# Fourier mixing, a dense layer and routed experts on one core: the experts as one list of token groups, routing in finer steps

## The chip, the cores and the metric

The kernel runs on one core of a Trainium2 chip. Its engines take their own queues of instructions: TensorE (PE in the profile) makes matrix products into PSUM banks, VectorE (DVE), ScalarE (ACT) and GpSimd (POOL) work element by element, SyncE (SP) issues most loads. ACT and POOL issue DMAs too. The metric is the device time of one execution in microseconds (us); the number compared is the median of several runs.

## What is computed

```python
def reference(x, w_r, w_i, b_r, b_i, moe_w_in, moe_w_out, w_gate, w1, w2, capacity):
    X = np.fft.rfft(x, axis=1)                                # x: 8 x 3072 x 256
    Yr = X.real @ w_r - X.imag @ w_i + b_r
    Yi = X.real @ w_i + X.imag @ w_r + b_i
    Y = shrink(Yr, 0.01) + 1j * shrink(Yi, 0.01)              # soft threshold
    y = np.fft.irfft(Y, n=3072, axis=1).reshape(-1, 256)
    h = y @ moe_w_in                                          # 256 -> 2048
    t = np.where(h > 0, h, np.exp(np.minimum(h, 0)) - 1) @ moe_w_out
    logits = t @ w_gate                                       # 8 experts
    e = logits.argmax(1); gate = softmax(logits)[e]
    # in token order an expert takes its first `capacity` = 768 tokens, the rest give 0
    out[i] = gate[i] * (np.maximum(t[i] @ w1[e], 0) @ w2[e])  # 256 -> 1024 -> 256
```

Products are made in split form: each operand is a sum of two narrower numbers, and three products stand for one.

## The kernel before

Three stages follow each other and overlap at their seams. The **Fourier stage** (to about 250 us) transforms and mixes three batches; its last inverse products (`fi`, line 268, taken out of PSUM by ACT as `yt`, line 269) run on beside the dense stage. With this data 55 tiles of 128 tokens fill all experts, so that only these are worked on (a tail for other data follows behind a branch that is not taken here).

The **dense stage** (class `Moe`) takes the 55 tiles as 14 chunks, 13 of four tiles and a last one of three, and 16 steps a chunk: 224 dense steps, counted by `g` in the main loop. A step is `up` (six products `pa`, line 453, of 512 columns, 384 in the last chunk) for step `g` and `down` (twelve products `pm`, line 476, nine in the last chunk) for step `g - 3`. Between them ACT makes two activations `e` (457, 458), DVE the third `e` (459), ACT the first half `g` (460) and DVE, or POOL in some steps, the second half (461). The PSUM banks of `pa` are three, and the DVE `e` frees one. At a chunk's end ACT copies `pm` to `row` (484).

**Routing** of a chunk is the generator `finish(c)`: each `next` on it puts down one portion. It makes 32 `lw` on DVE (504: one logit of 128 tokens each), then small DVE operations `mx`, `eq`, `sb`, `qi` and `oh` (515 to 522, the choice of the expert), `bf` and `al` on POOL (528: sums over the tiles), then three small products `pk` on PE (538, 539: places of the tokens), which take a bank of the three called `pd`, shared with `pm` of odd chunks, `fi` and the turns of the experts. From `pk` DVE makes `pg`, `cnt` (the running counts) and at last `sl`, by which POOL scatters the rows of each tile to the table `tab` in DRAM (helper line 395). For the last chunk the third tile is computed aside: POOL makes two `pr` (498) and ACT eight `la` from them (501), since the PE no longer needs ACT as much there.

The **expert stage** (class `Experts`) has eight experts of 768 rows, two groups of three tiles each. `load_x` loads an expert's rows `er` from `tab` through SP; `turn` transposes a tile on PE (`eturn`, 626) and splits it into two `ex` (ACT 628, DVE 629); `up` makes eight `eup` per group (646, six products each), from which ACT and DVE make `eh` (647, 648); `down` makes three `edown` (659, 24 products each), from which ACT makes `eo` (662), scattered by POOL to `out`. `split_w` splits the loaded weights `ewraw` into `ew` (606, 607) and issues a later load. `pieces` lists all of an expert's `up` of both groups, then its six `down`, with the splits and turns of the next expert between them.

The order on each engine is set by a scheduler that goes over the pieces as the loop emits them and moves instructions within reach of it; each engine then runs its list in that order. So the place of `next(steps)` or of a piece in the loop decides, but not alone.

Of the kernel before, what the change touches and what calls it, by code (L numbers as in the profile page):

```python
# [10 lines left out]
F32 = mybir.dt.float32  # L11
F32R = mybir.dt.float32r
BF16 = mybir.dt.bfloat16
I32 = mybir.dt.int32
# [24 lines left out]

W_AT, ROW_AT, TURN_AT = 7, 10, 4  # L40
LAG = 3
RW = 258
# [371 lines left out]
class Moe:  # L414
# [70 lines left out]

    def finish(self, c):

# [6 lines left out]
        for t in range(2, nt) if aside else ():  # L494

            for q in (0, 4):
# [59 lines left out]
class Experts:  # L556
# [53 lines left out]

    def load_x(self, e):
        t = self.tile("row", [128, self.st, RW], F32, "er")
        rows = self.tab[bass.ds((self.at + e) * self.slots, self.slots), :]
        load(self.tc, t, rows.rearrange("(t p) w -> p t w", p=128))
        self.row[e] = t

    def turn(self, e, g, t):

        nc = self.nc
        a, n = self.groups[g]  # L620
        if t == 0:
            pool = next(self.pools["x"])
            self.xt[e, g] = [pool.tile([128, 2, n * 128], F32R, name=f"ex{r}") for r in (1, 2)]
        ps = self.bank("turn", [128, 2, 128])
        for dh in range(2):
            nc.tensor.transpose(ps[:, dh, :], self.row[e][:, a + t, dh * 128:dh * 128 + 128], self.id)  # L626
# [23 lines left out]
    def down(self, e, g, t):  # L650
        nc = self.nc
        a = self.groups[g][0] + t
# [7 lines left out]
        row = self.row[e]  # L660
        o = self.tile("o", [128, D], F32, "eo")
        nc.scalar.activation(o, ps, AF.Copy, scale=row[:, a, D:D + 1])  # L662
        scatter(self.tc, "out", self.out, row[:, a, D + 1:D + 2].bitcast(I32), o, NT, self.free)

    def pieces(self, experts):

        out, ng, last = [], len(self.groups), experts[-1]
        turns = lambda e: [lambda g=g, t=t: self.turn(e, g, t) for g in range(ng) for t in range(self.groups[g][1])]
        for e in experts:
            todo = []  # L670
            if e < last:
                todo += [lambda e=e, i=i: self.split_w(e + 1, i) for i in range(4)]
                todo.insert(0 if e == experts[0] else len(todo), lambda e=e: self.load_x(e + 1))
                todo += turns(e + 1)
            first = e == experts[0]
            if first:
                out += turns(e)
                self.hold = todo[0] if todo else None
            n = 0
            for g in range(ng):  # L680
                for f in range(NFE):
                    out.append(lambda e=e, g=g, f=f: self.up(e, g, f))
                    n += 1
                    if first and todo and n == W_AT:
                        out.append(lambda: [self.load_w(q) for q in range(4, 7)])
                    if todo and (n > ROW_AT and len(todo) > len(turns(e)) if first else f % 2):
                        out.append(todo.pop(0))
            for g in range(ng):
                for t in range(self.groups[g][1]):
                    for _ in range(1 if not first else 0 if g * self.groups[0][1] + t < TURN_AT else 2):  # L690
                        if todo:
                            out.append(todo.pop(0))
                    out.append(lambda e=e, g=g, t=t: self.down(e, g, t))
            out += todo
        return out


@with_exitstack
def kernel(ctx, tc, x, w_r, w_i, b_r, b_i, moe_w_in, moe_w_out, w_gate, w1, w2, cst, out, cap):
# [154 lines left out]
    n = n_static * NF  # L854
    z0 = n // 3

    ex = Experts(tc, w1, w2, tab, out, slots, rt["id"])
# [4 lines left out]
    for g in range(n + 16):  # L862
# [14 lines left out]
        if not todo and left is not None:  # L877
            left.close()
            left = None
            pools = {m: [mk(fast, "e0_" + m, b)] * b for m, b in dict(raw=3, w=1, row=1, x=1, h=1).items()}  # L880
            tags = dict(turn=["pd"], up=["pa"], down=["pb", "pc"])
# [17 lines left out]
        if sp0 and g % 4 == 3:  # L899
            sp0.pop(0)()  # L900
        if g == n:

            snap = rtp.tile([1, 1], I32, name="snap")
            nc.vector.tensor_scalar(snap, rt["cnt"][0:1, 0:1], float(cap), None, op0=ALU.is_lt)
            ex.load_x(0)
            spx = ex.pieces(range(E))
        if g == n + LAG:
            mst.close()
            right.close()
            for m, b in dict(w=1, row=1, x=2, h=1, o=4).items():  # L910
                pools[m] = [mk(fast, "e1_" + m, b, side="right")] * b + pools.get(m, [])
            ex.phase(ps, tags, **pools)
            mp["pr"] = mk(fast, "e1_pr", 2, side="right")
        c -= 1
        if c >= 0 and f >= LAG:
            if f == LAG:
                steps = moe.finish(c)
            next(steps, None)
            if c == n_static - 2 and f == 5 or c == n_static - 1 and f > 5:
                next(steps, None)  # L920
        for _ in range(2):
            if g >= n + LAG and (spx[0] is not ex.hold or f > 10):
                spx.pop(0)()
    for _ in steps:
        pass
# [4 lines left out]
    nc.vector.tensor_tensor(more, more, snap, op=ALU.max)  # L930
    for piece in spx:
        piece()
    fast.close()
    with tc.If(nc.values_load(more[0:1, 0:1], min_val=0, max_val=1) > 0):
        tail(tc, mk, rt, (x, w_r, w_i, b_r, b_i, cst), (zs[0], vs[0], ys[0]), (moe_w_in, moe_w_out), tab, cap, slots)
        with tc.For_i(0, E, 1) as e, ExitStack() as again:
            pools = {m: [mk(again, "r_" + m, b)] * b for m, b in dict(raw=3, w=1, row=1, x=2, h=2, o=2).items()}
# [5 lines left out]
            ex.load_x(0)  # L943
            for i in range(4):
                ex.split_w(0, i)
            for piece in ex.pieces([0]):
                piece()
# [96 lines left out]
```

## Time and profile before

| | us |
|---|---|
| median of three runs (1234.79 to 1238.55) | 1236.99 |
| the profiled execution, its own time | 1233.33 |
| its span, first to last instruction | 1231.4 |
| PE busy | 1167.1 |
| DVE busy | 835.3 |
| ACT busy | 717.7 |
| POOL busy | 294.3 |
| mean granted clock of PE | 0.981 |

Busy time of an engine is the sum of its instructions. PE is close to the span, so one reads where it was idle and who ended that idle time (its releaser). A second thing to read is the granted clock of a stretch: 1.00 is 2.4 GHz, 0.50 is 1.2 GHz, and a stretch with a value between spent a part of its time at the lower level.

### The profile page before, as it was taken

The numbers are of one execution on the slowest core, as the hardware profiler recorded it, in microseconds if no ns is written. First come the engines' busy times: TensorE is split into PE (matmuls) and PEld (weight loads), VectorE is DVE, ScalarE is ACT, GpSimd is POOL, SyncE is SP. The second block draws the span as 40 slices with busy tenths as digits, with TensorE's granted clock in tenths as the row PEclk, the third lists the DMA queues.
The fourth block names the chain that finished last, engine by engine and source line by source line (L and its number), as shares of the span: only waits on it lengthen the run. The fifth ranks groups of instructions, "written<-read, shape, count | busy, mean of one in ns | idle before, by whom it ended". The sixth has DMA issues, their size and how long they took to land.

```text
span 1231.4 us, 20925 instructions
## 1 busy us (share of the span) xinstructions
PE 1167.1 (95%) x7656; PEld 1061.6 (86%) x7656; DVE 835.3 (68%) x2140; ACT 717.7 (58%) x1397; POOL 294.3 (24%) x335
## 2 busy tenths in 40 slices
PE   7888898999999999999999999999997999999994
PEld 2676798889999989999998899999987999999994
DVE  1699889873868768668588787788787544355430
ACT  4565676666666666666667566666655544355430
POOL 1234334311131231321212312312222111111111
PEclk9999998999999999999999999999998999999998
DMA  8965887555120211333424223212103522332100
GB/s 267 315 221 173 241 256 219 173 162 170 48 67 27 74 50 40 121 108 97 137 84 145 72 69 121 95 56 83 62 8 97 198 101 92 105 112 99 45 26 29
DMA packets 122784, 143.65 MB, mean 117 GB/s; under 512 B 8962, under 2 KB 106099, under 8 KB 122544
## 3 DMA queue, kind: packets, MB, share of 16 engines
q1 hardware_dynamic: 72688, 77.62, 20.8%
q10 hardware_dynamic: 45040, 51.96, 12.5%
q0 software_dynamic: 4944, 12.64, 2.9%
q8 instruction: 62, 1.02, 0.3%
q14 instruction: 50, 0.41, 0.1%
HBM read 71.96 MB, written 71.15 MB: 116 GB/s over the span
## 4 chain that ended last, share of the span: by engine, by line
PE 65%; DVE 8%; issue 4%; ACT 2%; DMA 2%; POOL 1%; POOLq 0%; SPq 0%; ACTq 0%; DVEq 0%
PE pm L476 22%; PE pa L453 22%; PE eup L646 9%; PE edown L659 8%; DVE lw L504 3%; PE fi L268 2%; DVE e L459 1%; DVE tc L237 1%; PE eturn L626 1%; POOL out L395 1%; DMA ewraw<-in_moe_w 1%; DVE g L461 1%; PE fmix L226 0%; ACT e L458 0%; PE fi L245 0%
## 5 line engine op out<-in xcount | busy, mean ns | idle before, releaser
L476 PEld LDWEIGHTS pm<-wout,g 128*128 128x128 f32 x2640 | 347.4, 192 | 18.3 <-ACT e L457 0.7
L476 PE MATMUL pm<-wout,g 128*128 128x256 f32 x2640 | 353.9, 283 | 0.5 <-DVE g L461 0.5
L453 PE MATMUL pa<-x,win 128*128 128x512 f32 (+1 forms) x1344 | 347.8, 394 | 1.0 <-DVE e L459 0.6
L453 PEld LDWEIGHTS pa<-x,win 128*128 128x128 f32 x1344 | 238.5, 190 | 38.9 <-DVE e L459 1.0
L460 ACT CAST g<-e 128x512 fp32r<-128x512 f32 (+1 forms) x224 | 136.7, 612 | 148.8 <-DVE e L459 147.9
L504 DVE SCALAR_TENSOR_TENSOR lw<-row,wg 128x256 bf16<-128x256 f32 x432 | 210.0, 486 | 12.1 <-ACT row L484 4.4
L459 DVE SCALAR_TENSOR_TENSOR e<-pa,e 128x512 f32<-128x512 f32 (+1 forms) x224 | 151.0, 677 | 86.4 <-ACT e L458 85.8
L461 DVE TENSOR_TENSOR g<-e,g 128x512 fp32r<-128x512 f32 (+1 forms) x182 | 139.3, 768 | 55.6 <-ACT g L460 53.6
L457 ACT ACTIVATE e<-pa 128x512 f32<-128x512 f32 (+1 forms) x224 | 132.4, 591 | 55.0 <-PE pa L453 54.1
L458 ACT ACTIVATE e<-e 128x512 f32<-128x512 f32 (+1 forms) x224 | 139.3, 625 | 4.9
L646 PE MATMUL eup<-ex,ew 128*128 128x384 f32 x768 | 141.3, 341 | 0.1
L659 PE MATMUL edown<-ew,eh 128*128 128x256 f32 x1152 | 139.8, 280 | 0.8 <-ACT eo L662 0.8
L659 PEld LDWEIGHTS edown<-ew,eh 128*128 128x128 f32 x1152 | 136.2, 188 | 1.0 <-ACT eo L662 1.0
L461 POOL TENSOR_TENSOR g<-e,g 128x512 fp32r<-128x512 f32 (+1 forms) x42 | 53.7, 1280 | 341.5 <-ACT g L460 302.4
L646 PEld LDWEIGHTS eup<-ex,ew 128*128 128x128 f32 x768 | 133.4, 189 | 1.6 <-DVE eh L648 0.6
L648 DVE SCALAR_TENSOR_TENSOR eh<-eup,eh 128x384 fp32r<-128x384 f32 x128 | 70.5, 555 | 54.0 <-ACT eh L647 53.9
L395 POOL DMA_INDIRECT out<-eo,er x48 | 46.6, 971 | 220.7 <-ACT ex L628 136.7
L647 ACT ACTIVATE eh<-eup 128x384 fp32r<-128x384 f32 x128 | 63.2, 494 | 57.6 <-PE eup L646 56.2
L237 DVE SCALAR_TENSOR_TENSOR tc<-tt,kb 64x256 f32<-64x256 f32 x144 | 81.6, 567 | 14.8 <-ACT kb L232 12.5
L607 DVE TENSOR_TENSOR ew<-ewraw,ew 128x512 fp32r<-128x512 f32 x64 | 42.1, 686 | 61.4 <-ACT ew L606 49.7
L662 ACT ACTIVATE eo<-edown,er 128x256 f32<-128x256 f32 x48 | 22.8, 475 | 94.3 <-PE edown L659 62.9
L395 POOL DMA_INDIRECT tab<-row,sl x55 | 57.7, 1050 | 51.7 <-DVE sl L551 39.2
(124 smaller groups left out, 1237.3 us busy)
## 6 DMA issues: line engine op xcount, KB each, us to landing
out<-row ACTq DMA_DIRECT2D x48, 512.0 KB, 3.4
ewraw<-in_moe_w SPq DMA_DIRECT2D x29, 512.0 KB, 4.5
xp<-in_x SPq DMA_DIRECT2D x24, 384.0 KB, 5.0
zs<-zo ACTq DMA_DIRECT2D x24, 384.0 KB, 4.0
zi<-zs SPq DMA_DIRECT2D x36, 256.0 KB, 5.1
vs<-vo ACTq DMA_DIRECT2D x36, 256.0 KB, 3.7
vi<-vs SPq DMA_DIRECT2D x48, 192.0 KB, 3.7
y<-ys SPq DMA_DIRECT2D x26, 256.0 KB, 3.4
```

Of the source, the lines that this page charges most:

```text
L237: nc.vector.scalar_tensor_tensor(c[b, j, :], t[a, r, :], 0.0, kb[a, r, :], op0=ALU.max, op1=ALU.subtract)
L395: i = tc.nc.gpsimd.indirect_dma_start(dst, bass.IndirectOffsetOnAxis(idx, 0), src, None, bounds_check=rows - 1, oob_is_err=False)
L453: nc.tensor.matmul(ps, l, r, start=n == 0, stop=n == len(ops) - 1)
L457: nc.scalar.activation(e, ps, AF.Exp)
L458: nc.scalar.activation(e, e, AF.Relu, bias=1.0, scale=-1.0)
L459: nc.vector.scalar_tensor_tensor(e, ps, 0.0, e, op0=ALU.max, op1=ALU.subtract)
L460: nc.scalar.copy(g1, e)
L461: (nc.gpsimd if f % 4 == 3 and f < NF - 1 else nc.vector).tensor_tensor(g2, e, f32(g1), op=ALU.subtract)
L476: nc.tensor.matmul(self.pm[c][h][:, o, :], l[:, ts], r[f // 2][:, f % 2, :], start=f == 0 and o == 0 and n == 0, stop=f == NF - 1 and (o = ...
L504: v.scalar_tensor_tensor(T("lw", [128, D], BF16), row[:, t, 0:D], 1.0, rt["wg"][:, e, :], op0=ALU.mult, op1=ALU.mult, accum_out=pl[:, t, e ...
L646: nc.tensor.matmul(ps, l, r, start=i == 0, stop=i == len(ops) - 1)
L659: nc.tensor.matmul(ps, l[:, f, ts], r[:, f, :], start=f == 0 and i == 0, stop=f == NFE - 1 and i == 2)
```

## The change

Three things, all in the order and the size of the pieces.

- `finish(c, per)` yields after every three `lw` (four in the last three chunks) in place of eight, so that a chunk's routing lasts longer and reaches into the next chunk's; a list `live` holds the routings under way and each is stepped once per dense step.
- The experts' work is one list over 16 groups. `load_x` loads the rows of one group (387 KB in place of 774 KB, two buffers). The three `down` of a group stand among the eight `up` of the next one, with the turns of the group after that and two splits; each piece has a cost (`up` 1, `down` 3, others 0) and the loop emits 2 per step.
- The handover: twelve steps before the dense stage ends the rows of expert 0 are loaded, and the three turns of its first group stand at the steps `n - 8`, `n - 5`, `n - 2`. The rows of group (1,1), the second of expert 1, are the first that must wait for every chunk's routing (`hold`). Two counters are kept at the early load, so that data for which the early load would be too early goes to the tail.

```diff
-    def finish(self, c):
+    def finish(self, c, per=E):
...
-        for t in range(nt):
-            for e in range(E) if t < 2 or not aside else ():
-                v.scalar_tensor_tensor(T("lw", [128, D], BF16), row[:, t, 0:D], 1.0, rt["wg"][:, e, :],
-                                       op0=ALU.mult, op1=ALU.mult, accum_out=pl[:, t, e:e + 1])
-            yield
+        last = (2 if aside else nt) * E - 1
+        for n in range(last + 1):
+            t, e = divmod(n, E)
+            v.scalar_tensor_tensor(T("lw", [128, D], BF16), row[:, t, 0:D], 1.0, rt["wg"][:, e, :],
+                                   op0=ALU.mult, op1=ALU.mult, accum_out=pl[:, t, e:e + 1])
+            if n % per == per - 1 or n == last:
+                yield
...
-    def load_x(self, e):
-        t = self.tile("row", [128, self.st, RW], F32, "er")
-        rows = self.tab[bass.ds((self.at + e) * self.slots, self.slots), :]
+    def load_x(self, e, g):
+        a, n = self.groups[g]
+        t = self.tile("row", [128, self.groups[0][1], RW], F32, "er")[:, 0:n, :]
+        rows = self.tab[bass.ds((self.at + e) * self.slots + a * 128, n * 128), :]
...
     def pieces(self, experts):
...
+        todo = [(e, g) for e in experts for g in range(len(self.groups))]
+        size = lambda k: self.groups[todo[k][1]][1]
...
+        out, self.hold = turns(0), None
+        for k, (e, g) in enumerate(todo):
+            side = {f: [] for f in range(NFE)}
+            if k + 1 < len(todo):
+                rows = (0, lambda k=k: self.load_x(*todo[k + 1]))
+                late = k == 2
+                if late:
+                    self.hold = rows
+                if k:
+                    side[ROW_AT if late else 0].append(rows)
+                for t, f in enumerate(turns(k + 1)):
+                    side[NFE - 1 if late else NFE - 1 - size(k + 1) + t].append(f)
+                split = []
+                if g == len(self.groups) - 1:
+                    split = [(e + 1, 0), (e + 1, 1)]
+                elif g == 0 and k:
+                    split = [(e, 2), (e, 3)]
+                for n, q in enumerate(split):
+                    side[2 * n + 1].append((0, lambda q=q: self.split_w(*q)))
+            for f in range(NFE):
+                out.append((1, lambda e=e, g=g, f=f: self.up(e, g, f)))
+                out += side[f]
+                if k and f % 3 == 1:
+                    t = f // 3
+                    if t < size(k - 1):
+                        out.append((3, lambda k=k, t=t: self.down(*todo[k - 1], t)))
...
+    TURN_AT = [n - 8, n - 5, n - 2]
+    live = []
...
-        if g == n:
-            snap = rtp.tile([1, 1], I32, name="snap")
-            nc.vector.tensor_scalar(snap, rt["cnt"][0:1, 0:1], float(cap), None, op0=ALU.is_lt)
-            ex.load_x(0)
+        if g == n - NF + LAG + 1:
+            while len(live) > 1:
+                step(0)
+            snap = rtp.tile([1, 2], I32, name="snap")
...
+            for q in range(len(ex.groups)):
+                ex.load_x(0, q)
             spx = ex.pieces(range(E))
...
-        if c >= 0 and f >= LAG:
-            if f == LAG:
-                steps = moe.finish(c)
-            next(steps, None)
-            if c == n_static - 2 and f == 5 or c == n_static - 1 and f > 5:
-                next(steps, None)
-        for _ in range(2):
-            if g >= n + LAG and (spx[0] is not ex.hold or f > 10):
-                spx.pop(0)()
+        for q in range(len(live)):
+            step(0)
+        if c >= 0 and f == LAG:
+            live.append(moe.finish(c, 3 if c < n_static - 3 else 4))
+            step(-1)
+        if c == n_static - 1 and f > 5:
+            step(-1)
+        if g == n - 8:
+            for q in range(4, 7):
+                ex.load_w(q)
+        room = 2 if g >= n else g in TURN_AT
+        while room > 0 and spx and (spx[0] is not ex.hold or not live):
+            cost, piece = spx.pop(0)
+            piece()
+            room -= cost if g >= n else 1
```

Three places show what the scheduler makes of it. Line numbers of after run two or three higher. PE, the `pk` of chunk 12 (the last chunk but one): before, inside the `up` of the last chunk's fourteenth step, with six `down` still to come.

```order
L453 MATMUL pa<-x,win_79 128x384 x2
L538 LDWEIGHTS u
L538 MATMUL pk<-oh,u 128x32
L453 MATMUL pa<-x,win_80 128x384
L538 LDWEIGHTS one
L538 MATMUL pk<-bf,one 128x32
L476 MATMUL pm<-wout_1795,g_10928 128x256
```

And after, behind the `down` of the last dense step but one:

```order
L476 MATMUL pm<-wout_1799,g_11047 128x256
L540 LDWEIGHTS u
L540 MATMUL pk<-oh,u 128x32
L540 LDWEIGHTS one
L540 MATMUL pk<-bf,one 128x32
L541 LDWEIGHTS one
L541 MATMUL pk<-al,one 128x8
L649 MATMUL eup<-ex_10868,ew_7677 128x384
```

It moved from the fourteenth `up` of the last chunk to the end of its `down`, among the first `eup`.

DVE, the last `lw` of chunk 12, which lie beside the dense steps of the last chunk (`e` frees a bank of `pa`, `g` is its second half). Before:

```order
L459 SCALAR_TENSOR_TENSOR e<-pa,e 128x384
L504 SCALAR_TENSOR_TENSOR lw,pl<-row,wg 128x256 x2
L461 TENSOR_TENSOR g_10929<-e,g_10928 128x384
L504 SCALAR_TENSOR_TENSOR lw,pl<-row,wg 128x256
L459 SCALAR_TENSOR_TENSOR e<-pa,e 128x384
L504 SCALAR_TENSOR_TENSOR lw,pl<-row,wg 128x256 x2
L515 TENSOR_REDUCE mx<-pl 128x4
```

After:

```order
L505 SCALAR_TENSOR_TENSOR lw,pl<-row,wg 128x256 x4
L459 SCALAR_TENSOR_TENSOR e<-pa,e 128x384
L505 SCALAR_TENSOR_TENSOR lw,pl<-row,wg 128x256
L632 TENSOR_TENSOR ex_10869<-eturn,ex_10868 128x2x128
L461 TENSOR_TENSOR g_10839<-e,g_10838 128x384
L505 SCALAR_TENSOR_TENSOR lw,pl<-row,wg 128x256 x10
L517 TENSOR_REDUCE mx<-pl 128x4
L518 TENSOR_TENSOR eq<-pl,mx 128x32
L519 TENSOR_TENSOR sb<-pl,mx 128x32
L522 TENSOR_TENSOR eq<-eq,e_2362 128x32
L523 TENSOR_REDUCE qi<-eq 128x4
L524 TENSOR_TENSOR oh<-qi,e_2362 128x32
```

One or two `lw` stood between two operations of the dense step; now ten stand together, and the next `e` behind `oh`.

ACT in the handover, where `row` of the last chunk, the `la` of its third tile, `ex` of the turns and `eh` of the first `eup` meet. Before:

```order
L484 COPY row<-pm 128x256
L501 ACTIVATE la,pl<-pr 128x256 x2
L628 CAST ex_11187<-eturn 128x2x128
L501 ACTIVATE la,pl<-pr 128x256
L628 CAST ex_11187<-eturn 128x2x128
L501 ACTIVATE la,pl<-pr 128x256
```

After (here `ex` is that of the second group of expert 0; `pr` stands on POOL right behind the four scatters of chunk 12 in both):

```order
L650 ACTIVATE eh_11103<-eup 128x384 x2
L501 ACTIVATE la,pl<-pr 128x256
L650 ACTIVATE eh_11103<-eup 128x384
L501 ACTIVATE la,pl<-pr 128x256 x2
L631 CAST ex_11183<-eturn 128x2x128
L501 ACTIVATE la,pl<-pr 128x256
L631 CAST ex_11183<-eturn 128x2x128
L501 ACTIVATE la,pl<-pr 128x256
L631 CAST ex_11183<-eturn 128x2x128
```

`la` stood among the `ex` of the first group and now stands among those of the second, with `eh` of the first between them.

## Rows read from the trace of the kernel before

**Rows 1.** Windows of 25 us: busy us per engine (instructions), clock, DMA share, GB/s.
```profile
675.00:700.00 25.00, 21.73 (x126) 18.98 (x125) 21.02 (x69) 14.38 (x26) 7.26 (x10) 0.93 0.18 62
...
900.00:925.00 25.00, 22.18 (x149) 21.46 (x147) 18.30 (x69) 13.46 (x29) 7.19 (x11) 0.93 0.06 14
925.00:950.00 25.00, 18.16 (x105) 16.89 (x106) 20.97 (x71) 12.45 (x38) 8.59 (x8) 0.86 0.27 96
```

**Rows 2.** PE waits, 250 to 1231 us: line, releaser, total, times, longest.
```profile
PE eturn L626 <- DVE ex L629: 3.9, 1, 3.9
PE pk L538 <- DVE oh L522: 3.8, 2, 2.2
PE eturn L626 <- DMA er<-tab: 2.8, 1, 2.8
PE pk L538 <- ACT yt L269: 2.3, 1, 2.3
PE pk L538 <- POOL bf L528: 1.9, 3, 1.1
...
PE edown L659 <- ACT eo L662: 0.8, 1, 0.8
```

**Rows 3.** Timeline of PE, 885 to 892 us: start us, us, what, shapes, count.
```profile
886.58 1.21 PE L453 MATMUL pa<-x,win 128*128 128x384 f32 x6
887.62 1.59 PE L476 MATMUL pm<-wout,g 128*128 128x256 f32 x12
889.05 1.21 PE L453 MATMUL pa<-x,win 128*128 128x384 f32 x6
```

**Rows 4.** Chain of waits behind three holes: start us, us, what.
```profile
693.40 2.37 PE pa L453 x6
...
914.94 1.28 PE pm L476 x8
916.22 1.92 PE pa L453 x6
...
935.27 3.06 PE eup L646 x15
...
938.56 4.26 PE eup L646 x24
```

**Rows 5.** Chain of waits on DVE, 909 to 914 us.
```profile
909.34 0.47 DVE g L461
...
911.00 0.44 DVE lw L504 x2
...
913.25 0.11 DVE oh L522
```

**Rows 6.** Chain of waits, 943 to 975 us.
```profile
948.81 2.32 DMA tab<-row,sl
...
951.73 5.59 DMA ewraw<-in_moe_w
...
965.65 2.83 PE edown L659 x24
```

**Rows 7.** Timeline of POOL, 911 to 934 us; idle time ahead in brackets.
```profile
917.00 1.06 POOL L395 DMA_INDIRECT tab<-row,sl  x1 [2.09 <-DVE sl L551]
...
920.92 1.01 POOL L395 DMA_INDIRECT tab<-row,sl  x1 [0.30 <-issue]
925.62 4.82 POOL L498 TENSOR_TENSOR pr<-wg,row 128x1024 f32<-128x1024 f32 x2 [3.69 <-ACT row L484]
```

**Rows 8.** Costliest groups of the page: busy us, mean ns, idle ahead.
```profile
L648 DVE SCALAR_TENSOR_TENSOR eh<-eup,eh 128x384 fp32r<-128x384 f32 x128 | 70.5, 555 | 54.0 <-ACT eh L647 53.9
...
L607 DVE TENSOR_TENSOR ew<-ewraw,ew 128x512 fp32r<-128x512 f32 x64 | 42.1, 686 | 61.4 <-ACT ew L606 49.7
```

**Rows 9.** Timeline of ACT, its first `la`.
```profile
927.99 0.42 ACT L501 ACTIVATE la<-pr 128x256 bf16<-128x256 f32 x1 [2.45 <-POOL pr L498]
```

**Rows 10.** Timeline of DVE beside the first `pr`.
```profile
925.77 2.47 DVE L504 SCALAR_TENSOR_TENSOR lw<-row,wg 128x256 bf16<-128x256 f32 x1
```

More of the change, by code (lines that the diff above doesn't have):

```diff
@@ L659, in down @@
                 nc.tensor.matmul(ps, l[:, f, ts], r[:, f, :], start=f == 0 and i == 0, stop=f == NFE - 1 and i == 2)
-        row = self.row[e]
+        row = self.row[e, g]
         o = self.tile("o", [128, D], F32, "eo")
-        nc.scalar.activation(o, ps, AF.Copy, scale=row[:, a, D:D + 1])
-        scatter(self.tc, "out", self.out, row[:, a, D + 1:D + 2].bitcast(I32), o, NT, self.free)
+        nc.scalar.activation(o, ps, AF.Copy, scale=row[:, t, D:D + 1])
+        scatter(self.tc, "out", self.out, row[:, t, D + 1:D + 2].bitcast(I32), o, NT, self.free)
@@ L665, in pieces @@
     def pieces(self, experts):
[L667 to L694, printed above, removed]
@@ L695, in pieces, with turns @@
-        return out
+        todo = [(e, g) for e in experts for g in range(len(self.groups))]
+        size = lambda k: self.groups[todo[k][1]][1]
+        def turns(k):
+            return [(0, lambda t=t: self.turn(*todo[k], t)) for t in range(size(k))]
+        out, self.hold = turns(0), None
[24 more added lines that the diff above has]
+                        out.append((3, lambda k=k, t=t: self.down(*todo[k - 1], t)))
+            if k:
+                out += [(3, lambda k=k, t=t: self.down(*todo[k - 1], t)) for t in range(3, size(k - 1))]
@@ L698 @@
+        k = len(todo) - 1
+        return out + [(3, lambda t=t: self.down(*todo[k], t)) for t in range(size(k))]
 @with_exitstack
@@ L855, with step @@
     z0 = n // 3
+    TURN_AT = [n - 8, n - 5, n - 2]
+    live = []
+    def step(i):
+        if live:
+            s = live.pop(i)
+            if next(s, live) is not live:
+                live.append(s)
     ex = Experts(tc, w1, w2, tab, out, slots, rt["id"])
@@ L879 @@
             left = None
-            pools = {m: [mk(fast, "e0_" + m, b)] * b for m, b in dict(raw=3, w=1, row=1, x=1, h=1).items()}
+            pools = {m: [mk(fast, "e0_" + m, b)] * b for m, b in dict(raw=3, w=1, row=2, x=1, h=1).items()}
             tags = dict(turn=["pd"], up=["pa"], down=["pb", "pc"])
@@ L909 @@
             right.close()
-            for m, b in dict(w=1, row=1, x=2, h=1, o=4).items():
+            for m, b in dict(w=1, row=2, x=2, h=1, o=4).items():
                 pools[m] = [mk(fast, "e1_" + m, b, side="right")] * b + pools.get(m, [])
@@ L914 @@
         c -= 1
-        if c >= 0 and f >= LAG:
-            if f == LAG:
-                steps = moe.finish(c)
-            next(steps, None)
-            if c == n_static - 2 and f == 5 or c == n_static - 1 and f > 5:
-                next(steps, None)
-        for _ in range(2):
-            if g >= n + LAG and (spx[0] is not ex.hold or f > 10):
-                spx.pop(0)()
-    for _ in steps:
-        pass
+        for q in range(len(live)):
[13 more added lines that the diff above has]
+            room -= cost if g >= n else 1
+    while live:
+        step(0)
     more = rtp.tile([1, 1], I32, name="more")
@@ L929 @@
     nc.vector.tensor_reduce(more, room, axis=AX.X, op=ALU.max)
-    nc.vector.tensor_tensor(more, more, snap, op=ALU.max)
-    for piece in spx:
+    for q in range(2):
+        nc.vector.tensor_tensor(more, more, snap[:, q:q + 1], op=ALU.max)
+    for _, piece in spx:
         piece()
@@ L936 @@
         with tc.For_i(0, E, 1) as e, ExitStack() as again:
[L937 removed]
+            pools = {m: [mk(again, "r_" + m, b)] * b for m, b in dict(raw=3, w=1, row=2, x=2, h=2, o=2).items()}
             ex = Experts(tc, w1, w2, tab, out, slots, rt["id"])
@@ L942 @@
                 ex.load_w(q)
-            ex.load_x(0)
+            for q in range(len(ex.groups)):
+                ex.load_x(0, q)
             for i in range(4):
                 ex.split_w(0, i)
-            for piece in ex.pieces([0]):
+            for _, piece in ex.pieces([0]):
                 piece()
```

12 lines of the change are left out of this document (7 added, 5 removed).

## The prediction

> **What bounds the kernel now.** I read the stretches first. TensorE (PE) sets the end: in nearly every 25 us stretch from 250 us to the last product it is busy without a gap, and the short ones are 425 to 450 us, by one hole, 950 to 975 us, by 0.8 us, and the three in [rows 1]. 675 to 700 us and 900 to 925 us have a granted clock of 0.93, and 925 to 950 us, where the dense stage hands over to the experts, has 18.16 us of work at 0.86. So a change that leaves the number of products alone can give back only these holes. The list of waits [rows 2] names them: the small routing product `pk` waits 2.3 us for ACT `yt`, 3.8 us for `oh` on VectorE (DVE) and 1.9 us for `bf` on POOL; the first turn of the expert stage waits 2.8 us for its rows `er` and a later one 3.9 us for `ex`; an `edown` waits 0.8 us for `eo`. That is 15.5 us. Then the chain of waits, for what follows a hole: at full pace, from start to start, six `pa` of 384 columns take 1.04 us and twelve `pm` 1.43 [rows 3]. At 693.40 six `pa` of 512 columns take 2.37, where 4/3 of 1.04 is 1.39: 1.0 us lost, and by the same rate about 0.6 on the `pm` behind them. At 914.94 eight `pm` take 1.28 (0.95 at full pace) and six `pa` 1.92: 1.2 us, and about 0.4 on the nine `pm` behind [rows 4]. Of the first `eup` of the experts fifteen take 3.06, where twenty-four at full pace take 4.26, so fifteen 2.66; with the three ahead of them, slow too, about 0.8 [rows 4]. Only the hole before 448 us is followed by no slow products. **Ceiling of the gain: 15.5 + 4.0 = 19.5 us.** Everything else is the same products in another order.
>
> **What the change removes.** (1) *`pk` stands later.* In the order of before, `oh` of a chunk stands on DVE about four dense steps ahead of the `pk` on PE that reads it, and one step or less at the two chunks where `pk` waits for it. The order of after has `oh` at the same dense steps, but `pk` 7 to 11 steps behind it. That is far more than the waits need: the last `lw`, `mx` to `oh` and `bf` take 3 to 4 us [rows 5], a step 2.5 [rows 3]. Price: 8.0 us back, with 3.2 us of low clock. The finer steps themselves hardly matter: the scheduler had spread `lw` between `e` and `g` already, and spreads them alike now. (2) *Rows and turns of expert 0 move into the dense stage.* Its loads are issued some twelve steps before the dense stage ends, when all earlier chunks are routed, and its turns stand between dense products. Neither the 2.8 nor the 3.9 us wait has its cause left, nor the 0.8 us of clock behind them. Price: 7.5 us. (3) The 0.8 us at `eo` came from a split that waited for weights queued behind a 774 KB row load [rows 6]; loads of half the size should remove it, but I count it at 0.4 (0 to 0.8). (4) Products of two groups interleaved: the stretches of the experts are full already, so nothing to win. Its cover must hold, though: each `down` now stands one group after its `eh`, which is more room than before. Gain: 8.0 + 6.7 + 0.4 + 4.0 = **19.1 us**.
>
> **What it adds.** (a) *Ten `lw` in a row on DVE.* In the last dense chunk the order of after puts, between two `e` that free PSUM banks of `up`, eleven `lw`, an `ex`, a `g` and `mx` to `oh`. At 0.44 for an `lw`, 0.47 for a `g` or an `ex` and about 1.4 for `mx` to `oh` (from the last `lw` to the end of `oh` less an `e`) [rows 5] that is 4.8 + 0.9 + 1.4 + 0.5 for the `e` itself = 7.6 us between two `e`. PE needs one `e` per step, 2.1 us (1.04 and nine `pm` at 1.07), and holds three banks, so that it can run on for two steps less the microsecond that ACT takes first: 2.1 + 3.2 = 5.3. A hole of 2.3 us; if DVE comes late into it, behind the four `lw` that stand just ahead, up to 4; if the `e` before came early, 1. I take 2.5.
>
> (b) *POOL: four scatters ahead of `pr`.* For the last chunk POOL makes `pr`, from which ACT makes `la`. Before, the scatters of chunk 12 were over at 921.93, ahead of the last dense product, and `pr` began at 925.62 [rows 7]. In after `pk` of chunk 12 stands 2 `eup` and 9 `pm` ahead of the last dense product, 3.2 us; from `pk` to the scatter was 2.1 us before (914.9, where the `pm` behind it start, to 917.00 [rows 4, 7]), now with four `ew` (0.69) and two `eh` (0.56) among it on DVE [rows 8], so up to 6. The scatters start 1 us before to 2.8 us after the last dense product; they take 4.9 us, the two `pr` 4.8, and `la` starts 2.4 us behind the first [rows 7, 9]. ACT takes its work in the order that stands: the `ex` of all three turns of group (0,1) and two `eh` stand among the `la`, and the last `ex` behind the fifth, which needs the second `pr`. From scatters at 0 that is 4.9 + 4.8 + 0.4 for `la`, 0.4 for `ex` and 0.5 for its DVE half: 11.0 us after the last dense product (10 to 14). PE has four `eup` (4.2), three turns (0.7) and sixteen `edown` products (1.9, which want `eh` from the same ACT queue): 4.9 to 6.8. Hole: 3 to 8 us, and I take 5, since the early scatter needs only that DVE keeps its order while the late one needs every `ew` at full length. One row widens it: beside `pr` an `lw` took 2.47 us instead of 0.43 [rows 10], twice; in after `lw` stand between the three DVE halves of `ex`. The nearest rows put that at 0 to 2 us, inside the bounds. The Trainium skill (GPSIMD Engine Reference, section Specifications) says that GpSimd contends with DVE instructions that have two SBUF inputs; by it `lw` would be held for the whole of `pr` and `ex`, which reads PSUM, would not, and the hole would be nearer to 6 than to 5, the sum 1 us higher; the two slow `lw` agree, and no row has an `ex` beside a `pr`.
>
> (c) *A bank.* `pk` now falls into the middle of odd chunks, where two `pm` and the last inverse Fourier products (`fi`) share three banks; `fi` behind a `pk` must wait for `cnt` on DVE. The nearest row is the same contest the other way, 2.3 us [rows 2]; three such places stand in the order. 0 to 2.7, I take 1. (d) *Clock.* Two holes of the size of (a) and (b) are followed by slow products as in [rows 4], 0.8 to 1.6 us each: I take 2.6 (0 to 3.5). (e) Later snapshots, two more DVE instructions, the list's budget: a few tenths on DVE beside PE work; zero. Sum: 2.5 + 5 + 1 + 2.6 = **11.1 us** (4 to 18).
>
> **Sum.** 11.1 - 19.1 = -8.0. The profiled execution took 1233.3 us, with 1231.4 of span; the median of the runs is 1237.0, so the profiled one is a quick one. I put the change on the median: **1229 us**; by the bounds 1222 to 1236.
>
> **Rivals.**
> *Holes covered.* DVE and POOL run far enough ahead, (a) is under 1 us, (b) at 3 and no slow clock follows: cost 4, gain 15, 1222 us. For it: DVE is idle for a quarter of 900 to 925 us [rows 1], so it may reach the ten `lw` early. Against: the order lets no `e` pass them.
> *The handover is as bad as before.* (a) 4, (b) 8, 2.7 of bank and 3.5 of clock: 18, 1236. For it: 925 to 950 us shows that one late chain costs 7 us there, and POOL, DVE and ACT orders chain in the same way.
> *Slower: rows of (1,1) late.* This group is the first to need every chunk routed. The chain of (b) goes on: from `pk` of chunk 13 it is 2.1 us to the scatters as in (b), three of them 3.6, their landing 2.3, the issue 0.6, and the load at most the 5.6 us that twice the size took beside weights [rows 6, 7]: 14.2, or 18 with the DVE work of (b) in front. The order has nine `eup` (1.07) and three `edown` of 24 products (2.8) between that `pk` and the turn, 18.1 us of PE [rows 4, 6]. The margin is 0 to 4. If it is gone the turn blocks PE's queue and each further us costs one. At 6 us late beside the ends of (a) to (d), 24 against 19: 1242. It decides once (b) and the late rows together pass 12 us.
> *It doesn't do what it says.* The finer routing steps leave DVE's order as it was. If `oh` came so late that the moved `pk` still waits, 8.0 + 3.2 of the gain are gone and the sum is +3: 1240. Against: 7 steps of distance are 17 us.
>
> **Chances.** Forecast (1224 to 1233) 0.52; covered 0.14; as bad as before 0.18; late rows 0.11; no effect on `pk` 0.05. Runs of this kernel can tell 0.3% (3.7 us) from no change: faster is below 1233.3, same to 1240.7. Faster: the forecast, the covered case and a little of the third (1236 with its spread), 0.67; same: the rest of the third and most of the last, 0.20; slower 0.13. The range reaches from 1219, just past the covered case, to 1240, which leaves out the late rows.
>
> **What would show it.** Right: no `pk` among PE's waits; first turn without a wait; a PE hole of 2 to 3 us at an `up` of the last chunk, released by DVE `e`, and one of 4 to 6 us at an `eup` or turn of group (0,1), released by `ex`; clock below 1 only there. Wrong: holes at other places, above all a turn that waits for `er`; `pk` still waiting; or a stretch of the experts that is no longer full.

## The result and the profile after

The changed kernel takes 1224.61 us (median, 1220.98 to 1226.02), against 1237.53 for the kernel before in the same runs: ratio 0.9895, 95% interval 0.9868 to 0.9921, a gain of 12.9 us. The forecast was 1229, a gain of 8.

The profiled executions (1233.33 and 1224.62 us) differ by 8.7. Part of the gap to 12.9 is the Fourier stage: the first `pa` came between 243.6 and 248.6 us in the profiled executions of all kernels below, though that stage's code is the same in all (before 244.4, after 246.3). So kernels are compared by two stretches, each from one starting product to another in the trace: *dense*, first `pa` to last `pm`, and *experts*, last `pm` to last `edown` (16.2 to 16.3 us more to the end in all of the table; sums are rounded last). Each stretch is that of the one profiled execution. In after, four `eup` and three turns, 4.8 us, lie in the dense stretch.

| kernel | median us | dense | experts | sum |
|---|---|---|---|---|
| before | 1237.5 | 680.3 | 290.5 | 970.8 |
| after | 1224.6 | 678.5 | 281.9 | 960.4 |
| coarse | 1232.4 | 686.7 | 278.7 | 965.4 |
| coarse_late | 1229.0 | 682.6 | 282.0 | 964.6 |
| old_hand | 1228.8 | 675.3 | 286.7 | 962.0 |
| routing_only | 1227.2 | 670.8 | 291.0 | 961.8 |
| own_downs | 1224.8 | 678.8 | 281.1 | 959.9 |
| loads_on_sp | 1220.9 | 674.2 | 282.5 | 956.7 |
| no_aside | 1216.2 | 678.5 | 274.6 | 953.0 |
| half_aside | 1222.1 | 674.3 | 282.2 | 956.5 |
| both | 1214.4 | 674.3 | 276.0 | 950.2 |
| both_own | 1224.1 | 675.2 | 285.4 | 960.6 |
| before_no_aside | 1232.3 | 681.5 | 287.2 | 968.8 |

PE's waits in after, 250 us to the end (line, releaser, total us, times, longest), answer to [rows 2]; two Fourier waits are left out:

```profile
PE eup L649 <- ACT ex L631: 4.7, 1, 4.7
PE pa L453 <- DVE e L459: 3.5, 1, 3.5
...
PE fi L268 <- PE pa L453: 0.8, 1, 0.8
PE fi L268 <- issue: 0.7, 1, 0.7
```

None of the six waits of [rows 2] is left, and neither are three short ones that it does not show, two of `pa` for `e` (0.6 us) and one of `pm` for `g` (0.5); four new ones sum to 9.7 us. The windows (as [rows 1]) say the same: 675 to 700 us is full, the two at the seam are not.

```profile
675.00:700.00 25.00, 24.93 (x157) 22.33 (x157) 20.06 (x60) 15.27 (x28) 6.32 (x9) 1.00 0.18 60
...
900.00:925.00 25.00, 21.54 (x144) 21.25 (x143) 20.72 (x63) 15.27 (x36) 1.90 (x6) 0.93 0.18 64
925.00:950.00 25.00, 20.25 (x123) 19.88 (x122) 15.57 (x62) 11.96 (x38) 11.42 (x11) 0.86 0.34 116
```

Hole (a), timeline of PE and then that of DVE in after (start us, us, what; idle time ahead in brackets). The two `e` of the last chunk start 7.3 us apart (899.11 and 906.38; forecast 7.6), with the ten `lw` between them. DVE had no pause between the two. The products behind the hole are slow, and lose 1.7 us (`pm` 1.9 for nine in place of 1.07, `pa` 1.4 and 1.5 for 1.04, from start to start):

```profile
906.98 1.57 PE L453 MATMUL pa<-x,win 128*128 128x384 f32 x6 [3.46 <-DVE e L459]
908.35 2.13 PE L476 MATMUL pm<-wout,g 128*128 128x256 f32 x9
910.28 1.68 PE L453 MATMUL pa<-x,win 128*128 128x384 f32 x6
```

```profile
899.11 0.55 DVE L459 SCALAR_TENSOR_TENSOR e<-pa,e 128x384 f32<-128x384 f32 x1
...
904.91 0.42 DVE L505 SCALAR_TENSOR_TENSOR lw<-row,wg 128x256 bf16<-128x256 f32 x1
...
906.38 1.01 DVE L459 SCALAR_TENSOR_TENSOR e<-pa,e 128x384 f32<-128x384 f32 x2
```

Hole (b), the timelines of PE, POOL and ACT in after, one after the other; the last dense `pm` starts at 924.8:

```profile
936.48 1.01 PE L649 MATMUL eup<-ex,ew 128*128 128x384 f32 x2 [4.75 <-ACT ex L631]
```

```profile
925.64 1.00 POOL L395 DMA_INDIRECT tab<-row,sl  x1 [3.64 <-DVE sl L553]
...
930.58 4.68 POOL L498 TENSOR_TENSOR pr<-wg,row 128x1024 f32<-128x1024 f32 x2
```

```profile
933.00 0.42 ACT L501 ACTIVATE la<-pr 128x256 bf16<-128x256 f32 x1 [5.11 <-POOL pr L498]
...
936.06 0.37 ACT L631 CAST ex<-eturn 128x256 fp32r<-128x256 f32 x1
```

The first `pr` ends just ahead of 933.00, `la` and `eh` stand ahead of `ex`, and the last `ex` is made at 936.06. By the second stretch of slow products (30 `eup` and 8 `edown` products take 8.9 us where 6.2 are due) another 2.7 us are lost.

### The profile page after: what moved, and what is told of

Its sections match the earlier page's. It is cut to its first block, busy times and chain, and to the rows that moved or that the text cites. A ratio compares the mean times of both kernels' runs of the same rounds, so it can differ in the third digit from the quotient of the medians.

```text
span 1222.8 us, 20965 instructions
## 1 busy us (share of the span) xinstructions
PE 1162.1 (95%) x7656; PEld 1061.1 (87%) x7656; DVE 825.4 (67%) x2142; ACT 717.6 (59%) x1397; POOL 293.6 (24%) x335
## 4 chain that ended last, share of the span: by engine, by line
PE 51%; issue 19%; DVE 6%; POOL 4%; ACT 1%; DMA 1%; POOLq 0%; SPq 0%; ACTq 0%; DVEq 0%
PE pm L476 24%; PE pa L453 23%; POOL out L395 4%; PE fi L268 2%; DVE lw L505 2%; DVE tc L237 1%; DVE e L459 1%; PE eup L649 1%; DVE g L461 0%; POOL tab L395 0%; PE fi L245 0%; PE fmix L226 0%; DMA y<-ys 0%; DMA fv<-in_moe_w_out 0%; DVE tt L230 0%
## 5 line engine op out<-in xcount | busy, mean ns | idle before, releaser
L505 DVE SCALAR_TENSOR_TENSOR lw<-row,wg 128x256 bf16<-128x256 f32 x432 | 211.0, 488 | 12.9 <-ACT row L484 4.9
L461 DVE TENSOR_TENSOR g<-e,g 128x512 fp32r<-128x512 f32 (+1 forms) x182 | 128.4, 707 | 62.1 <-ACT g L460 58.7
L649 PE MATMUL eup<-ex,ew 128*128 128x384 f32 x768 | 150.9, 343 | 4.7 <-ACT ex L631 4.7
L661 PE MATMUL edown<-ew,eh 128*128 128x256 f32 x1152 | 143.6, 281 | 0.0
L661 PEld LDWEIGHTS edown<-ew,eh 128*128 128x128 f32 x1152 | 140.3, 189 | 0.0
L461 POOL TENSOR_TENSOR g<-e,g 128x512 fp32r<-128x512 f32 (+1 forms) x42 | 54.1, 1288 | 184.0 <-ACT g L460 112.2
L439 POOL TENSOR_TENSOR x<-y,x 128x512 fp32r<-128x512 f32 (+1 forms) x28 | 35.6, 1283 | 124.7 <-ACT x L438 124.5
```

The lines of the kernel that those rows point to most:

```text
L461: (nc.gpsimd if f % 4 == 3 and f < NF - 1 else nc.vector).tensor_tensor(g2, e, f32(g1), op=ALU.subtract)
L649: nc.tensor.matmul(ps, l, r, start=i == 0, stop=i == len(ops) - 1)
```

## Experiments

**coarse and coarse_late: is it the place of `pk` or the finer portions?**

```diff
-            live.append(moe.finish(c, 3 if c < n_static - 3 else 4))
+            live.append(moe.finish(c))                                      # coarse
+            live.append(moe.finish(c, E, 7 if c < n_static - 3 else 4))     # coarse_late
...
-    def finish(self, c, per=E):
+    def finish(self, c, per=E, rest=0):                                     # coarse_late
...
-        for _ in range(3):
+        for _ in range(3 + rest):                                           # coarse_late
             yield
```

> The changed kernel with one edit: every `finish` yields after eight `lw`, as before the change, so that `pk` stands about four dense steps behind `oh` again (in the order, at the dense steps 30, 46, ... where before had it). Theory (what pays is that `pk` stands later): the holes at `pk` of the chunk at 448 us (2.3 us, ACT `yt`) and of the one at 691 us (2.7 us, and 1.6 us of slow products) come back, the two short waits of `fi` go (1.5 us), so the dense stage from its first `pa` to its last `pm` is 683 to 685 us against 678.5 in the changed kernel; the scatters of chunk 12 come 3 us earlier, so the hole at the second group's `ex` shrinks from 4.7 to 2 to 4. Time 1226 to 1230. Rival (the finer portions of `lw` relieve DVE): holes at `up` or `down` released by DVE `e` or `g` in many chunks, 1231 to 1236.

> The changed kernel with `lw` in portions of eight, but with seven (in the last three chunks four) empty steps more ahead of `pk`, so that `pk` stands at the same dense steps as in the changed kernel. Theory (only the place of `pk` counts): no `pk` waits, the dense stage is 677.5 to 679.5 us, the time 1223 to 1227, the same as the changed kernel. Rival (the finer portions count): as slow as the kernel with coarse portions and early `pk`, 1228 to 1236.

Both were slower: 1232.4 and 1229.0 us (ratios to before 0.9959, interval 0.9942 to 0.9976, and 0.9929, 0.9908 to 0.9950). The time of coarse lies above its range and in that of the rival, whose holes in many chunks are not there; its profiled execution was its quickest run (1228.5), so the table shows it at its best. In coarse the holes of before in the fourth and the ninth chunk return to 0.01 us, here in the timeline of PE; the two waits of `fi` are gone, so these belong to the late `pk`:

```profile
449.19 0.18 PE L540 MATMUL pk<-oh,u 128*128 128x32 bf16 x1 [2.27 <-ACT yt L269]
```

In coarse_late no `pk` waits, yet the dense stretch is 4.1 us longer than after's (0.4 of it in the fourth chunk, 2.1 in the ninth, 1.3 in the last, by the starts of each chunk's first `pa`). The ninth has new holes, and the one of the last chunk is longer and followed by more slow products:

```profile
679.55 1.65 PE L453 MATMUL pa<-x,win 128*128 128x512 f32 x6 [0.70 <-DVE e L459]
...
682.36 1.46 PE L476 MATMUL pm<-wout,g 128*128 128x256 f32 x10 [0.92 <-POOL g L461]
...
910.62 2.29 PE L453 MATMUL pa<-x,win 128*128 128x384 f32 x6 [3.83 <-DVE e L459]
```

So of the 8.2 us that the routing gives in the dense stretch (coarse against after), half is the place of `pk` and half the finer portions, taken in this order. My theory held that the second is nothing; it fell.

**old_hand and routing_only: what is the early handover worth?**

```diff
-        if g == n - NF + LAG + 1:
+        if g == n:                                                          # old_hand
...
-    TURN_AT = [n - 8, n - 5, n - 2]
+    TURN_AT = []                                                            # old_hand
-        room = 2 if g >= n else g in TURN_AT
+        room = 2 if g >= n + LAG else 0                                     # old_hand
```

routing_only is the other half: the kernel before, with after's `finish`, `live` and `step`.

> The changed kernel with the old handover: the rows of expert 0 are loaded after the last `up` of the dense stage, its turns stand behind the last `down`, and its `up` start three steps later; routing and the interleaved list stay. Theory: the wait of the first turn for `er` (2.8 us) and the wait for `ex` (some 3 to 4 us) come back with slow products behind them (2 to 3 us); the hole at the second group's `ex` (4.7 us and 2.7 us of slow products) shrinks or merges with them; the hole at the `up` of the last chunk (3.5 us, DVE `e`) stays. From the last dense `pm` to the last `edown` 288 to 293 us against 282.1, less 4.8 us of expert work that moved out of the dense stage. Time 1226 to 1231. Rival (the early handover only changed one hole for another): within 2 us of the changed kernel, 1222.5 to 1226.5.

> The kernel before with the routing of the changed one alone: portions of three and four `lw`, several routings under way, `pk` 7 to 11 steps behind `oh`; rows, turns, experts' list and weight loads as before. Theory (the routing is worth its 11 us in the dense stage, and the early handover is what keeps its late `pk` from costing at the seam): chunks 0 to 12 take what they take in the changed kernel (635.1 us up to the last chunk's first `pa` less 5), the last chunk 39.5 to 41 us without the ten `lw`; but the scatters of chunk 12 now end 4 to 6 us behind the last dense `pm`, and the rows of expert 0 are loaded behind them, so the wait for `er` grows from 2.8 to 6 to 10 us and the stretch to the last `edown` from 290.5 to 293 to 299. Time 1225 to 1231. Rival (the parts add up, the handover does not depend on the routing): 290.5 us there, 1222 to 1225.

1228.8 us (0.9926, 0.9905 to 0.9946) and 1227.2 (0.9923, 0.9905 to 0.9942). By the two stretches the early handover is worth 1.6 us (the medians are 4.2 apart; the first `pa` of old_hand came 2.3 later), and the routing alone has 9.0 of the 10.4. In neither does a turn wait for `er`, and I had put that wait in both; the expert stretches lie 1.3 and 2.0 us below their ranges. The timeline of SP in routing_only shows why no turn waits: the load is issued 27 us ahead of the last `pm` (918.4); before it was issued at 923.32, behind the four scatters of chunk 12.

```profile
891.00 0.38 SPq L110 DMA_DIRECT2D er<-tab  x1
```

With the longer `finish` these scatters stand behind the load in the order, so that it no longer waits for them. With the routing alone the seam has other holes: an `edown` waits 3.5 us for `eh`, an `eup` 1.0. The handover of old_hand has short holes (0.56, 0.46, 1.39 and 1.80 us at turns and `eup`) and one at `pk` from the ten `lw`, which stayed; its list on PE has changed, so the hole is no longer at an `up`:

```profile
908.17 0.21 PE L540 MATMUL pk<-oh,u 128*128 128x32 bf16 x1 [3.16 <-DVE oh L524]
```

**loads_on_sp: where hole (a) comes from.** Why ten `lw` stand together cannot be read in the diff's routing: in the order they stand where ACT issues three weight loads, which ran for 1.34 us on ACT's queue at 899.70 (timeline of ACT in after):

```profile
899.70 1.34 ACTq L110 DMA_DIRECT2D ewraw<-in_moe_w  x3
```

```diff
-        eng = self.nc.scalar if 4 <= q < 7 else self.nc.sync
+        eng = self.nc.sync
```

> The changed kernel with one edit: the three loads of expert 1's weights (ewraw), which ACT issues eight steps before the dense stage ends, are issued by SP in their place. In the order the ten `lw` in a row on DVE are gone with it (two or three stand between two `e` again). Theory (the row of ten `lw` makes the hole of 3.5 us at the `up` of the last chunk): no wait of `pa` for DVE `e` there and no slow products behind it; the last chunk takes 43 to 44 us from its first `pa` to the last `pm` against 48.5 with the same four or five us of expert work in it, so 42.9 to 44.5 and the whole 1218 to 1221. Rival (DVE is late in the last chunk whatever its order, and the hole only moves, to `pk` or to the turns): 47 to 49 us for the last chunk or as much more behind it, 1223 to 1226.

1220.9 us (0.9873, 0.9856 to 0.9889). No `pa` waits in the last chunk, and where the ten `lw` stood DVE's order now has two at most between two operations of the dense step; the dense stretch is 4.3 us shorter, a little under the hole and its slow products (3.5 + 1.7). As DVE had no pause between the two `e` of after, it is the order on DVE, and not ACT's 1.34 us, that made the hole; why the scheduler makes that order stays open. Hole (b) grew to 5.6.

**no_aside, both, half_aside, no_scatter12: hole (b).** no_aside leaves out the pool `pr`, so that DVE makes all 24 `lw` of the last chunk; both adds loads_on_sp; half_aside (with loads_on_sp) makes one `pr` of the two; no_scatter12 leaves out chunk 12's scatters.

```diff
-            mp["pr"] = mk(fast, "e1_pr", 2, side="right")                  # no_aside, both
...
-            for q in (0, 4):
+            for q in (4,):                                                  # half_aside
-        last = (2 if aside else nt) * E - 1
+        last = (2 * E + 4 if aside else nt * E) - 1                         # half_aside
...
-        for t in range(nt):
+        for t in range(nt if c != len(self.tiles) - 2 else 0):              # no_scatter12
             scatter(self.tc, "tab", self.tab, sl[:, t:t + 1], row[:, t, :], E * self.slots)
```

> The changed kernel with the third tile of the last chunk routed on DVE like the others: 24 `lw` in place of 16, no `pr` on POOL and no `la` on ACT. Theory (the hole of 4.7 us at the second group's first `eup` comes from `pr` behind the four scatters, with `ex` behind `la` on ACT): the hole shrinks to 0 to 1.5 us, its slow products go too (2.7 us), the rows of group (1,1) come up to 4 us later for the eight `lw` but without a hole. From the last dense `pm` to the last `edown` 274.5 to 278.5 us against 281.9; time 1217.5 to 1221.5. Rival (DVE becomes the one that is waited for): holes of 3 us or more at `eup` released by DVE `eh` or `ex`, or a turn that waits for `er`; 280 us or more, 1223 to 1229.

> Both edits together: weights issued by SP, the third tile on DVE. Theory (two independent causes): the two gains add, 1212 to 1217. Rival (both holes are one and the same lateness of DVE): no better than the better of the two alone, 1217 to 1222.

> Weights issued by SP, and half of the third tile's logits aside: one `pr` on POOL with four `la`, four `lw` more on DVE. Theory (the hole is scatters, then two `pr`, then `la` ahead of `ex`): one `pr` less is 2.4 us less, the hole is 1.5 to 3 us and the time 1214.5 to 1219, between the whole aside and none. Rival (the hole is set by the scatters alone, or by ACT): as long as with two `pr`, 4 to 5 us, 1218 to 1221.

> The changed kernel without the four scatters of chunk 12 to `tab` (its 512 rows are left out, so that their slots stay empty); `pr` then stands on POOL with nothing ahead of it, and the order on ACT puts six `la` ahead of the first `ex`. Theory (the hole is set by the moment the first `pr` is made, behind 5 us of scatters): `pr` starts about 1 us behind the last dense `pm` in place of 5.8, the hole at the second group's first `eup` falls from 4.7 to 0.5 to 3 us. Rival (the line of `la` ahead of `ex` on ACT makes it by itself): 4 us or more.

no_aside: 1216.2 us (0.9836, 0.9820 to 0.9852; 1.3 us below its range), no hole at all in the expert stretch, which is 7.3 us shorter: 4.7 of hole and 2.7 of slow products. both: 1214.4 (0.9817, 0.9801 to 0.9834), the quickest kernel of the study, 10 us under after; the sums of the stretches fall by 3.7, 7.3 and together 10.1. Its waits of PE:

```profile
PE fi L268 <- PE pa L453: 0.8, 1, 0.8
PE fi L268 <- issue: 0.7, 1, 0.7
PE eup L649 <- DVE ex L632: 0.5, 1, 0.5
PE eup L649 <- DVE eh L651: 0.2, 1, 0.2
```

half_aside missed: 1222.1 us (0.9882, 0.9865 to 0.9898), the hole 5.5, both above the rival's figures too. Timelines of POOL and ACT: the first `la` starts as late as with two `pr` (9.5 us behind the last `pm`, which starts at 921.45; 9.6 in loads_on_sp), since it waits for the scatters and the *first* `pr`.

```profile
928.59 2.37 POOL L498 TENSOR_TENSOR pr<-wg,row 128x1024 f32<-128x1024 f32 x1
```

```profile
930.99 0.42 ACT L501 ACTIVATE la<-pr 128x256 bf16<-128x256 f32 x1 [6.42 <-POOL pr L498]
```

In no_scatter12 (1225.24 us, one execution) `pr` starts 1 us behind the last `pm` (926.93), as expected, but the hole is 3.2, just past the end of my range, at an `eup` that waits for DVE's half of an `eh`. ACT's half was made at 928.68; DVE was late, since beside the two `pr` an `lw` took 2.57 us and an `ew` 2.82, where 0.42 and 0.69 are usual (timelines of POOL, DVE and PE):

```profile
927.89 4.88 POOL L498 TENSOR_TENSOR pr<-wg,row 128x1024 f32<-128x1024 f32 x2 [3.71 <-ACT row L484]
```

```profile
930.49 2.82 DVE L609 TENSOR_TENSOR ew<-ewraw,ew 128x512 fp32r<-128x512 f32 x1
...
933.58 0.55 DVE L651 SCALAR_TENSOR_TENSOR eh<-eup,eh 128x384 fp32r<-128x384 f32 x1
```

```profile
934.18 2.29 PE L649 MATMUL eup<-ex,ew 128*128 128x384 f32 x6 [3.17 <-DVE eh L651]
```

So hole (b) needs `pr` at this place: behind the scatters it holds PE through `la` and `ex` on ACT, without them through DVE. coarse agrees with nothing left out: its scatters come ahead of the last `pm`, `pr` starts 1 us behind it, an `ew` takes 2.83 and the wait for `eh` is 3.2. The scatters add some 1.5 us to it, in an order that is made anew without them.

**own_downs and both_own: interleaving.**

```diff
-                if k and f % 3 == 1:
-                    t = f // 3
-                    if t < size(k - 1):
-                        out.append((3, lambda k=k, t=t: self.down(*todo[k - 1], t)))
...
+            out += [(3, lambda k=k, t=t: self.down(*todo[k], t)) for t in range(size(k))]
```

> The changed kernel with the interleaving undone: the three `edown` of a group stand behind that group's own eight `up`, everything else alike. Theory (the experts' stretches were full before, nothing to win): the period of an expert stays at 34.8 to 35.1 us and the time within 2 us of the changed kernel, 1222.5 to 1227; perhaps a wait at the first `edown` of a group for its last `eh`, up to 0.8 us where it occurs, in the first experts only. Rival (interleaving gives the cover that ACT and DVE need): a hole of 0.5 to 1 us in each of 16 groups, 1232 to 1240.

> The quickest so far (weights issued by SP, third tile on DVE) with the interleaving undone, the `edown` of a group behind its own `eup`. Theory (interleaving is worth nothing where the experts' stretches are full): 1213 to 1216, within 1.5 us of the same kernel with interleaving; a wait of the first `edown` of group (0,0) or (0,1) for its last `eh` of up to 2 us at the seam. Rival (with the holes gone the interleaving is what covers ACT and DVE there): 1217 to 1221.

On after it is worth nothing: 1224.8 us (0.9897, 0.9877 to 0.9917). On both it is worth 9.7: 1224.1 (0.9902, 0.9883 to 0.9921), beyond even the rival's range. The timeline of PE in both_own has two holes where groups (0,1) and (1,0) begin:

```profile
941.35 3.70 PE L649 MATMUL eup<-ex,ew 128*128 128x384 f32 x12 [2.80 <-DVE eh L651]
965.36 3.16 PE L649 MATMUL eup<-ex,ew 128*128 128x384 f32 x10 [3.17 <-DVE eh L651]
```

The two have different causes. Ahead of the first, DVE made eight `lw` in a row and the small routing operations behind them (936.48 to 940.75) before the `eh` that PE waited for. That all 24 `lw` are on DVE fits, but own_downs with no_aside alone was not run. Ahead of the second, DVE was idle: its `ew`, which stands ahead of the `eh`, waited for ACT's `ew`, and ACT for weights. SP had issued these at 956.41, behind two row loads; the first of them, the rows of (1,1), had waited 4.7 us for the last chunk's scatters (timelines of ACT and of SP):

```profile
963.49 0.62 ACT L608 CAST ew<-ewraw 128x512 fp32r<-128x512 f32 x1 [3.55 <-DMA ewraw<-in_moe_w]
```

```profile
955.36 0.95 SPq L110 DMA_DIRECT2D er<-tab  x2
956.41 0.98 SPq L110 DMA_DIRECT2D ewraw<-in_moe_w  x2
```

In the kernel both the same two loads of weights went out at 954.62, and nothing waited for them. So with the `edown` among the `eup` both places are covered. In own_downs the seam had two waits of 2.0 us (`edown` for `eh`) in place of (b), so the cover was not missed.

**before_no_aside: what `pr` costs DVE.** The same edit as no_aside, made to the kernel before.

> The kernel before with the third tile of the last chunk routed on DVE: 24 `lw` in place of 16, no `pr` and no `la`. Theory (beside `pr` DVE stands still: two `lw` took 2.47 and 2.44 us in place of 0.42, so that moving 8 `lw` aside to save 3.6 us of DVE cost it 4.1 there, at the worst moment): no `lw` above 0.6 us in the last chunk, the wait of a turn for `ex` falls from 3.9 to 0 to 1 us, from the last dense `pm` to the last `edown` 284 to 287 us against 290.5; time 1230 to 1234. Rival (the eight `lw` cost on DVE what `pr` cost, and the late rows of expert 1 cost more): 289 to 293 us, 1235 to 1239.

1232.3 us (0.9965, 0.9951 to 0.9979). The wait for `ex` fell from 3.9 us to 0.5 and the expert stretch to 287.2, 0.2 above its range, as the wait for `er` (2.8) stayed; no `lw` of the last chunk is slow (by tile: minimum, median and maximum in ns; before had a maximum of 2474):

```profile
L504 DVE SCALAR_TENSOR_TENSOR lw<-row,wg x24: 412/418/427, 927.4 to 944.4; 128x256 bf16<-128x256 f32 x24
```

## Why the prediction was right in its direction, and where its terms were off

- *What the change removes.* Right that all six waits go: 15.5 us. (1) was right on the hole at `pk` and wrong that "the finer steps themselves hardly matter": coarse_late shows 4.1 us. The order of `lw` between `e` and `g` looked alike, and that was too coarse a reading of it. (2) was credited wrongly: of its 7.5 us the early handover gives 1.6; the wait for `er` went with the longer routing, by the order of the load and the scatters.
- *The slow products of before* were put too low: 0.8 us at the first `eup`, but the turns there are slow too (four turn products took 1.36 us in the chain at 932.53 where 0.44 is due), so 2 or more.
- *(a)* 2.5 forecast, 3.5 measured (bounds 1 to 4). The distance of the two `e` was right (7.3, forecast 7.6); the cover was not, 3.8 in place of 5.3. The first of them started 0.9 us after ACT had made its input (898.24), behind the four `lw` that the upper bound names, one of which took 1.13 us. *(b)* 5 forecast, 4.7 measured, at the place named; but its last step was wrong: the second `pr` was over at 935.26 and the fifth `la` started at 935.65 straight behind an `ex`, so that ACT's own line behind the first `pr` set the end, as half_aside confirms. *(c)* 1 forecast, 1.5. *(d)* 2.6 forecast, 4.4 measured, past its bound of 3.5: 1.7 behind (a), about the 1.6 of the dearest hole of before, and 2.7 behind (b).
- *The sum*: costs 14.1 in place of 11.1, slow products of before 5 to 6 in place of 4; between the profiled executions -8.7 against -8.0. With the sizes as measured the terms give some 7 us (15.5 + 5.5 - 14.1), while the sum of the stretches fell by 10.4, so that 3.5 us are in no term. Of these 1.1 are the three short waits left out of the ceiling. Some 1.3 more, by an estimate, come from a hole's costing more than its idle time: twelve `pm` are on PE for 1.59 us but step by 1.43 [rows 3], so each hole takes 0.16 more, and there are eight fewer. The rest stays open. That the forecast came out 4.4 us from the median is luck in part: costs and gains were both put too low, and part of the gain was credited to the wrong edit. The median moved by 12.9. The profiled execution of before was a quick one by 4 us, 1.5 of which is the next section's hole without slow products; that the rest is the Fourier stage is likely, and was not shown, since only single executions have a trace.
- *Rivals.* No turn waited for the rows of (1,1) in any run; they show once, in both_own, where they held up the weights behind them. The 5.6 us that this rival took for a row load are in [rows 6] those of weights issued behind one. "Holes covered" and "as bad as before" did not happen: both holes came at their places. Interleaving was called worth nothing; on after that is right, and both_own shows that it does not hold once hole (a) and hole (b) are gone.

## What to carry to other kernels

When a change spreads work out, read the new order for the longest run of foreign instructions between two operations that free a buffer: its length in time, less what the buffers cover, gave the hole to about a microsecond (2.5 forecast, 3.5 measured). Ask then what put the run there; here it was the engine that issues three loads. A part that is worth nothing by itself may be the cover that the next removal needs, so try parts again once the holes beside them are gone. Work moved to POOL to spare DVE can hold DVE instead: leaving `pr` out gave 4 us in before.

## What was not expected of the hardware

The hole ahead of `pk` in the fourth chunk is 2.3 us in before, coarse and before_no_aside. In before full pace went on behind it; in the other two the products were slow and the chunk took 54.2 and 54.1 us against 52.6. The chains of waits, first of before and then of coarse:

```profile
448.71 1.49 PE pa L453 x6
```

```profile
449.41 2.61 PE pa L453 x6
452.02 1.86 PE pm L476 x12
```

The granted clock of 425 to 475 us was 1.00 in before and 0.97 in coarse, so a part of that stretch ran at 1.2 GHz. The same idle time is thus followed by a fall in one execution and not in another; what decides stays open.

Beside `pr` DVE made no headway in before: two `lw` of 2.47 and 2.44 us [rows 10], and none slow once `pr` was gone. In coarse and no_scatter12 an `ew` beside `pr` took 2.8 us in place of 0.69. The Trainium skill (GPSIMD Engine Reference, section Specifications) says that GpSimd contends with DVE instructions that have two SBUF inputs, which `lw` has; the runs agree. An `eh`, which reads PSUM, kept its 0.56 us beside the second `pr` of after (933.92). In the last chunk of after, one `lw` of the sixteen was slow, 1.16 us. Not only `pr` does it: all 26 `lw` of before that took over 0.6 us, of 432, ran beside a `pr` or a half `g` made by POOL.
